# Row sums in SBUF, column mixing in one go, a later norm, a last tile in parts and a reordered first batch, in an attention-and-mixer kernel

## The chip, the cores and the metric

The kernel runs on one core of a Trainium2 chip. The metric is the device time of one execution in microseconds (us), as the median of several runs. Beside it stand profiles: one execution each, with every instruction of every engine. The engines are PE (matrix products), PEld (PE's weight loads), DVE (the vector engine), ACT (the scalar engine), POOL (GpSimd) and SP, which here only issues transfers. A profile's span is about 1.8 us shorter than the time of the same run, so spans are compared with spans and times with times.

Each run also lists its mean granted PE clock, where 1.000 is full speed.

## The reference, cut to what matters

Eight batches, each with 12 heads, 448 tokens and 64 numbers per head, so 768 columns per token:

```python
q_n, k_n = rmsnorm(q, g_q), rmsnorm(k, g_k)        # over the 64 numbers of a head
attn = softmax(q_n @ k_n^T / 8)
x    = heads side by side of attn @ v              # (8, 448, 768)
u    = x + (x^T @ U @ V)^T                         # "mixing": rank 32, over tokens
out  = u + relu(u @ w_ch1) @ w_ch2                 # "MLP": 768 -> 3072 -> 768
```

## The kernel before: the parts that matter

One stream of PE work carries everything. While PE makes the two MLP products of batch b (`ph`, then `po`), the pieces of batch b + 1 (scores, exponentials, values, then the mixing) are woven between its matmuls. Only batch 0 has no MLP to hide behind: its order is written out by hand in a string, HEAD. A "pair" is two heads of a batch; six pairs make a batch, so pairs 12 and 13 open batch 2.

Row sums of squares go into one PSUM bank. The logarithm and the exponential work in place there, and the scaling reads the result:

```python
rs_bank = ps_r.tile([SP, 6 * 16], FP32, name="rs_bank")      # PSUM
def reduce(p, hs=ALL):
    nc.vector.tensor_reduce(rs_of(p)..., sqs[p]..., AX, OP.add)
def rsqrt(p, n=1):
    rs = rs_of(p, n)
    nc.scalar.activation(rs, rs, AF.Ln, bias=eps)
    nc.scalar.activation(rs, rs, AF.Exp, scale=-0.5)
def scale(p):
    ...  # qkn = qk * rs_of(p), one DVE instruction of 112 x 1024
```

The mixing multiplies x by U in two column halves. In each, four matmuls of 32 output rows run side by side on four strips of the array (in the mixing of batch 3 they start within 0.01 us, from 230.39). All the large products share a pool of three PSUM buffers:

```python
ps_mm = ctx.enter_context(tc.tile_pool(name="ps_mm", bufs=3, space=bass.MemoryType.PSUM))
def mix_t(b, cols):
    t4 = t_of(b)
    for c in cols:
        pm = ps_mm.tile([P, c.stop - c.start], FP32, tag="mm", name="pm")
        mix_to(pm, b, c)
        nc.vector.tensor_copy(t4[:, c], pm)
def mixing(b):
    items = [(1, lambda h=h: mix_t(b, [slice(h * HALF, (h + 1) * HALF)])) for h in range(2)]
    for i in range(3 + b % 2):
        for half in range(2):
            items.append((1, lambda i=i, half=half: mix_x(b, i, half)))
    ...
```

The second MLP product writes 384 columns at a time, DVE adds x, and a whole tile of 128 tokens is stored at once on SP's queue:

```python
for i, half in order:
    po = ps_mm.tile([P, HALF], FP32, tag="mm", name="po")
    for hc in range(KH):                    # KH = 24
        nc.tensor.matmul(po, hT[:, hc, i * P:(i + 1) * P], w2b[:, half, hc], ...)
    nc.vector.tensor_add(osb[:, hs], po, xt[i][:, hs])
    if half == 1:
        store(b, off, off + P, osb, 0)      # two nc.sync.dma_start
```

The kernel begins with idle products on zeros, `heat(NWARM, ...)`, and HEAD has more of them (`F1:2` means one such product, into bank 2). The other words are steps too: `sq1:a` squares pair 1 on ACT, `R1` its row sums, `q1` its root, `S1` its scaling, `SC00` scores, `X00` an exponential.

The softmax here doesn't subtract the row's maximum and nothing guards it: scores larger than these inputs give would overflow.

Of the kernel before, what the change touches and what calls it, by code (L numbers as in the profile page):

```python
# [9 lines left out]
FP32 = mybir.dt.float32  # L10
# [7 lines left out]
def kernel(  # L18
# [20 lines left out]
    P = 128  # L39
# [14 lines left out]
    def segments(c0, c1):  # L54
        c = c0
        while c < c1:
            j, p = divmod(c, SP)
            n = min(SP - p, c1 - c)
            yield j, p, p + n, c - c0
            c += n  # L60
# [24 lines left out]
    eps = consts.tile([SP, 1], FP32, name="eps")  # L85
    rk0 = consts.tile([SP, 8], FP32, name="rk0")
    NE, NV, NQ, NWARM = 2, 3, 4, 12
    Es = [consts.tile([SP, 2, PAD + NJ * S + PAD], BF16, name=f"E{i}") for i in range(NE)]
# [11 lines left out]

    def rs_of(p, n=1):

        c = 16 * (p % 6)
        return rs_bank[:, c:c + 16 * n]

# [110 lines left out]
    def reduce(p, hs=ALL):  # L216
        nc.vector.tensor_reduce(rs_of(p).rearrange("p (s h j) -> p s h j", s=2, h=2)[:, :, hs],  # L217
                                sqs[p].rearrange("p (s h j d) -> p s h j d", s=2, h=2, d=D)[:, :, hs], AX, OP.add)

    def rsqrt(p, n=1):  # L220
        rs = rs_of(p, n)
        nc.scalar.activation(rs, rs, AF.Ln, bias=eps)
        nc.scalar.activation(rs, rs, AF.Exp, scale=-0.5)  # L223
# [103 lines left out]
    def t_of(b):  # L327
        if b not in t4s:
            t4s[b] = upool.tile([P, dm], BF16, tag="t4b", name="t4b", bufs=3)
        return t4s[b]  # L330

    def mix_to(pm, b, c):
        xt = x_tiles(b)
        for i in range(4):
            nc.tensor.matmul(pm[i * rank:(i + 1) * rank, :], Ub[:, b % 2, i, :], xt[i][:, c],  # L335
                             start=True, stop=True)

    def mix_t(b, cols):
        t4 = t_of(b)
        for c in cols:  # L340
            pm = ps_mm.tile([P, c.stop - c.start], FP32, tag="mm", name="pm")
            mix_to(pm, b, c)
            nc.vector.tensor_copy(t4[:, c], pm)
# [23 lines left out]
    def mixing(b):  # L367
        items = [(1, lambda h=h: mix_t(b, [slice(h * HALF, (h + 1) * HALF)])) for h in range(2)]
        for i in range(3 + b % 2):
            for half in range(2):  # L370
                items.append((1, lambda i=i, half=half: mix_x(b, i, half)))
            items.append((0, lambda i=i: turn_u(b, i)))
        return items

    def store(b, c0, c1, osb, r0):
        orow = out[b].rearrange("(p j) d -> j p d", j=NJ)
        for j, p0, p1, r in segments(c0, c1):
            nc.sync.dma_start(orow[j, p0:p1, :], osb[r0 + r:r0 + r + p1 - p0, :])

    def mlp(b):  # L380
# [19 lines left out]
        if b == 0:  # L400
            order = [(i, half) for half in range(2) for i in range(3)]
        for i, half in order:
            off = OFFS[par][i]
            if i not in osbs:
                osbs[i] = opool.tile([P, dm], FP32, tag="osb", name="osb")
            osb = osbs[i]
            hs = slice(half * HALF, (half + 1) * HALF)
            po = ps_mm.tile([P, HALF], FP32, tag="mm", name="po")
            for hc in range(KH):
                nc.tensor.matmul(po, hT[:, hc, i * P:(i + 1) * P], w2b[:, half, hc],  # L410
                                 start=(hc == 0), stop=(hc == KH - 1))
                if hc % 6 == 5 and hc != KH - 1:
                    yield HALF
            nc.vector.tensor_add(osb[:, hs], po, xt[i][:, hs])  # L414
            if half == 1:
                if off < 0:
                    store(b - 1, 384, 448, osb, 0)
                    store(b, 0, 64, osb, 64)
                else:
                    store(b, off, off + P, osb, 0)  # L420
            yield HALF

    def attention(b):
        items = []

        def add(weight, fn, *args):
            items.append((weight, lambda: fn(*args)))

        for p in range(b * 6, b * 6 + 6):
# [21 lines left out]
            if t + 2 < NT:  # L451
                for a in range(2):
                    if odd and p > 10:
                        add(0, reduce, 2 * t + 4 + a if p > 11 else 12 + a)
                    elif not odd and not early:
                        add(0, squares, 2 * t + 4 + a)
# [24 lines left out]
            if p == 9:  # L481
                add(0, touch, 6)
                add(0, load, 6)
                add(0, load_v, 6)
            if odd and p > 10 and t + 2 < NT:
                add(0, rsqrt, 2 * t + 4 if p > 11 else 12, 2)
        add(1, values, b * 6 + 5, 0)
# [24 lines left out]
    def begin(hcs, dcs):  # L512
# [17 lines left out]
    HEAD = """  # L530
        sq00:a R00 sq01:a q00 R01 q01 rk00 rk01 Sq00 G Sk0 Sq01 GC Tq0:0 Sl0 sq2:p Tk0:1 F1:2
        Tl0:2 sq3:p sq1:a Eq0 R1 Ek0:a SC00 F3:0 El0:v q1 cast0 S1 X00 SC01 F2:0 R2 sq4:p SC02
        T1:0 w10 X01 SC03 F3:1 X02 q2 Eq1 X03 Ek1:v w11 S2 SC10 F1:0 SC11 X10 T2:0 R3 SC12 late
        sq5:p X11 V01:1 Ek2:v Eq2 SC13 cast1 V00:0 q3 N01 X12 X13 w12 SC20 S3 X20 w13 SC21 T3:1
        R4 SC22 X21 sq6:p q4 V11:2 X22 SC23 Eq3 Ek3:v N00 V10:1 cast2 SC30 X23 S4 pU:0 N10 SC31
        N11 X30 X31 T4:1 R5 Ub:a SC32 V20:2 Eq4 SC33 X32 Ek4:v X33 q5 w14 N20 V21:0 N21 MT0:1
        SC40 X40 MT1:2 SC41 t1:a V31:0 t0:v MU0:1 S5 N31 X41 u0:v SC42 T5:2 X42 MT2:0 Eq5 SC43
        V30:1 Ek5:v SC50 X43 R6 t2:a MU1:2 SC51 X50 sq7:p N30 V40:0 X51 SC52 X52 u1:v MT3:1
        MU2:2 SC53 N40 X53 w15 V41:0 t3:v B10 R7 MU3:1 q6 u2:a u3:a N41 B00 V51:0 V50:2 B11
        MT4:1 w20 B01 B12 S6 t4:a N51 MU4:0 N50 MT5:1 w21 t5:a u4:a B02 B13 MU5:1 B03 u5:a S7  # L540
        B14 B04 B15 B05
    """

    def head():
# [3 lines left out]
        copies = {"a": nc.scalar.copy, "v": nc.vector.tensor_copy}  # L548
        rs0 = [rs_bank[:, 0:8], rsb[0:SP, 0, 0:8]]
        FIRST, REST = slice(0, 1), slice(1, NJ)  # L550

# [11 lines left out]
        def op(name, p, n, how):  # L563
# [5 lines left out]
            elif name == "R":  # L569
                if p == 0:  # L570
                    src = sqs[0].rearrange("p (s h j d) -> p s h j d", s=2, h=2, d=D)[:, :, n]
                    nc.vector.tensor_reduce(rs0[n].rearrange("p (s j) -> p s j", s=2), src, AX, OP.add)
                else:
                    reduce(p)
            elif name == "q" and p == 0:
                nc.scalar.activation(rs0[n], rs0[n], AF.Ln, bias=eps)
                nc.scalar.activation(rs0[n][:, 0:4], rs0[n][:, 0:4], AF.Exp, scale=-0.5)
# [85 lines left out]
    with tc.manual_schedule():  # L663
# [4 lines left out]
        load_pair(nc.sync, 0, 0, 1)  # L668
        load_pair(nc.scalar, 0, 1, 1)
        nc.scalar.preload_act_table_set("natural_log_exp_and_others")  # L670
# [15 lines left out]
        for b in range(B):  # L686
            fill = mlp(b)
            if b == 0:
# [12 lines left out]
                squares(15)  # L701
                weave(fill, volume(0) * 0.135, mixing(1))
                for a in range(2):
# [42 lines left out]
```

## Time and profile before

| | before |
|---|---|
| time, median of 3 runs | 593.5 us |
| span of the profile | 592.1 us |
| first `ph`, the start of batch 0's MLP | 39.67 us |
| first `po` row of 36 matmuls, just after the mixing of batch 1 | 98.39 us |
| last such row, just after the mixing of batch 7 | 519.02 us |

The last three rows are landmarks. The view of the critical chain joins neighbouring matmuls of one kind into a row, and after each mixing an unbroken row of 36 (odd batches) or 48 (even) `po` matmuls follows, so the start of this row tells to 0.01 us how far PE has come. They cut the span into the first batch, the stretch to the mixing of batch 1 (which holds the norm of batch 2), the steady part, and the tail.

Two more views of the kernel before, beside those that the prediction shows. First PE's waits, by what released them (columns: total us, times, longest), then the page's row of the wide row sums (busy us, mean ns of one, idle before them and its cause):

```profile
PE o L288 <- DVE xe L308: 1.5, 1, 1.5
PE sc L505 <- DVE xe L118: 1.3, 1, 1.3
PE sc L275 <- ACT qkT L250: 1.1, 1, 1.1
```

```profile
L217 DVE TENSOR_REDUCE rs_bank<-sq 112x16 f32<-112x1024 f32 x43 | 52.6, 1223 | 5.0 <-POOL sq L214 1.8
```

The first line is the wait in front of the mixing of batch 1. Its releaser is a small multiplication of DVE (it scales an output of the attention), but the second fence has the true cause: the row sums stood 1.8 us idle for squares of GpSimd, which had waited 1.85 us for a load.

### The profile page before, as it was taken

The numbers are of one execution on the slowest core, as the hardware profiler recorded it, in microseconds if no ns is written. First come the engines' busy times: TensorE is split into PE (matmuls) and PEld (weight loads), VectorE is DVE, ScalarE is ACT, GpSimd is POOL, SyncE is SP. The second block draws the span as 40 slices with busy tenths as digits, with TensorE's granted clock in tenths as the row PEclk, the third lists the DMA queues.
The fourth block names the chain that finished last, engine by engine and source line by source line (L and its number), as shares of the span: only waits on it lengthen the run. The fifth ranks groups of instructions, "written<-read, shape, count | busy, mean of one in ns | idle before, by whom it ended". The sixth has DMA issues, their size and how long they took to land.

```text
span 592.1 us, 11276 instructions
## 1 busy us (share of the span) xinstructions
PE 579.1 (98%) x4699; PEld 317.9 (54%) x4720; DVE 296.5 (50%) x599; ACT 263.3 (44%) x427; POOL 127.4 (22%) x112
## 2 busy tenths in 40 slices
PE   7999999999999999999999999999999999999996
PEld 3665555444655556544565556544565555554563
DVE  5967858454544566354453655454454452521111
ACT  6966530666305761366411774066620576113200
POOL 6946032333110332031130230302312000000000
PEclk9999999999999999999999999999999999999999
DMA  8999996925533445443154742641555210140011
GB/s 262 257 245 239 204 273 135 268 60 138 145 98 61 132 129 163 110 138 115 42 158 94 154 128 71 170 129 55 137 141 95 59 32 2 50 85 0 1 53 54
DMA packets 107955, 72.27 MB, mean 122 GB/s; under 512 B 56592, under 2 KB 104320, under 8 KB 107904
## 3 DMA queue, kind: packets, MB, share of 16 engines
q1 hardware_dynamic: 96336, 61.58, 39.8%
q0 software_dynamic: 11008, 9.44, 9.8%
q8 instruction: 37, 0.61, 0.4%
q10 hardware_dynamic: 560, 0.52, 0.3%
q14 instruction: 14, 0.11, 0.1%
HBM read 56.78 MB, written 11.01 MB: 114 GB/s over the span
## 4 chain that ended last, share of the span: by engine, by line
PE 91%; DMA 3%; DVE 3%; ACT 1%; issue 1%; SPq 0%; POOL 0%; DVEq 0%; POOLq 0%; ACTq 0%
PE ph L390 37%; PE po L410 36%; PE sc L275 7%; PE o L288 7%; DMA qk<-in_k_dram 2%; PE px L360 1%; DVE rs_bank L217 1%; DMA qk<-in_q_dram 1%; PE bank L288 1%; DVE qkn L228 1%; PE sc L520 1%; PE pm L335 1%; ACT E L280 0%; SPq L183 0%; ACT hT L393 0%
## 5 line engine op out<-in xcount | busy, mean ns | idle before, releaser
L280 ACT ACTIVATE E<-sc 112x896 bf16<-112x896 f32 x192 | 172.1, 914 | 157.0 <-PE sc L275 157.0
L410 PE MATMUL po<-w2b,hT 128*128 128x384 bf16 x1344 | 238.3, 326 | 0.0
L410 PEld LDWEIGHTS <-hT 128*128 128x128 bf16 x1344 | 126.4, 98 | 87.6 <-issue 9.0
L390 PEld LDWEIGHTS <-w1b 128*128 128x128 bf16 x1128 | 102.7, 98 | 105.2 <-issue 18.9
L214 POOL TENSOR_TENSOR sq<-qk 112x1024 f32<-112x1024 f32 x42 | 79.3, 1893 | 312.3 <-DMA qk<-in_k_dram 169.7
L390 PE MATMUL ph<-uB,w1b 128*128 128x512 bf16 x556 | 131.4, 379 | 1.1
L393 ACT ACTIVATE hT<-ph 128x512 bf16<-128x512 f32 (+1 forms) x122 | 66.7, 547 | 106.5 <-PE ph L390 106.0
L390 PE MATMUL ph<-uA,w1b 128*128 128x384 bf16 x552 | 100.3, 326 | 0.1
L395 DVE TENSOR_SCALAR hT<-ph 128x384 bf16<-128x384 f32 (+1 forms) x66 | 41.1, 622 | 90.4 <-PE ph L390 90.2
L288 PEld LDWEIGHTS <-E 112*128 112x128 bf16 x1536 | 60.8, 98 | 18.0 <-issue 3.2
L288 PE MATMUL o<-va,E 112*128 112x65 bf16 x1344 | 56.9, 194 | 1.5 <-DVE xe L308 1.5
L275 PE MATMUL sc<-qkT 64*128 64x448 bf16 x376 | 54.6, 355 | 1.6 <-ACT E L280 0.7
L228 DVE TENSOR_TENSOR qkn<-qk,rs_bank 112x1024 bf16<-112x1024 f32 x45 | 54.5, 1214 | 3.0 <-ACT rs_bank L223 2.6
L217 DVE TENSOR_REDUCE rs_bank<-sq 112x16 f32<-112x1024 f32 x43 | 52.6, 1223 | 5.0 <-POOL sq L214 1.8
L300 DVE RECIPROCAL rec<-o 128x4 f32<-128x4 f32 x84 | 15.2, 182 | 72.3 <-PE o L288 71.9
L414 DVE TENSOR_TENSOR osb<-po,xe 128x384 f32<-128x384 f32 x32 | 17.7, 557 | 40.2 <-PE po L410 39.6
L414 DVE TENSOR_TENSOR osb<-po,xo 128x384 f32<-128x384 f32 x24 | 13.4, 558 | 43.4 <-PE po L410 43.4
L275 PEld LDWEIGHTS <-qkT 64*128 64x128 bf16 (+1 forms) x384 | 13.3, 94 | 36.5 <-issue 28.2
L200 POOL CAST va<-vt 112x1024 bf16<-112x1024 f32 x23 | 23.9, 1040 | 2.7 <-DVE rs_bank L217 1.4
L266 ACT ACTIVATE qkT<-qkT,gg 128x448 bf16<-128x448 bf16 x36 | 23.8, 662 | 0.0
L362 DVE TENSOR_TENSOR xe<-px,xe 128x384 bf16<-128x384 f32 x32 | 17.7, 554 | 10.1 <-PE px L360 7.1
L308 DVE TENSOR_TENSOR xe<-o,rec 64x64 bf16<-64x64 f32 x84 | 18.3, 218 | 0.7
(92 smaller groups left out, 212.4 us busy)
## 6 DMA issues: line engine op xcount, KB each, us to landing
qk<-in_q_dram SPq DMA_DIRECT2D x44, 256.0 KB, 4.3
vt<-in_v_dram SPq DMA_DIRECT2D x22, 512.0 KB, 5.7
qk<-in_k_dram SPq DMA_DIRECT2D x43, 256.0 KB, 4.7
w1b<-in_moe_w_ch_dram POOLq DMA_DIRECT2D x6, 768.0 KB, 22.2
w2b<-in_moe_w_ch_dram POOLq DMA_DIRECT2D x6, 768.0 KB, 34.8
out_dram<-osb SPq DMA_DIRECT2D x8, 336.0 KB, 2.8
out_dram<-osb SPq DMA_DIRECT2D x8, 288.0 KB, 2.9
out_dram<-osb SPq DMA_DIRECT2D x8, 240.0 KB, 2.7
```

The source lines that it names most:

```text
L200: nc.gpsimd.tensor_copy(vas[t % NV][:, :, :, 0:D], v_of[t][0:SP].rearrange("p h (j d) -> p h j d", d=D))
L214: nc.gpsimd.tensor_tensor(dst, src, src, OP.mult)
L217: nc.vector.tensor_reduce(rs_of(p).rearrange("p (s h j) -> p s h j", s=2, h=2)[:, :, hs], sqs[p].rearrange("p (s h j d) -> p s h j d", s=2 ...
L228: nc.vector.tensor_tensor(qkns[p].rearrange("p j g d -> p g j d"), qk_of[t][0:SP, a].rearrange("p s h (j d) -> p (s h) j d", d=D), rs_of(p ...
L275: nc.tensor.matmul(sc[0:n, hh, 0:S], flat[pp, c:c + n], blocks(p)[pp, :, 0], start=True, stop=True)
L280: nc.scalar.activation(Es[p % NE][:, :, PAD + kc * S:PAD + (kc + 1) * S], scs.pop((p, kc))[0:SP, :, 0:S], AF.Exp, scale=float(D) ** 0.5)
L288: nc.tensor.matmul(o[:, i, :], E[:, hh, c:c + P], va[:, hl, kc, :], start=(kc == 0), stop=(kc == NJ - 1))
L390: nc.tensor.matmul(ph, w1b[:, dc, hc * P:(hc + 1) * P], u[:, dc, :], start=(dc == 0), stop=(dc == KD - 1))
L393: nc.scalar.activation(hT[:, hc, 0:n], ph, AF.Relu)
L395: nc.vector.tensor_relu(hT[:, hc, 0:n], ph)
L410: nc.tensor.matmul(po, hT[:, hc, i * P:(i + 1) * P], w2b[:, half, hc], start=(hc == 0), stop=(hc == KH - 1))
L414: nc.vector.tensor_add(osb[:, hs], po, xt[i][:, hs])
```

## The change

The intent has five parts, each of which removes a wait or shortens an end; no product is removed.

1. The row sums are written to an SBUF tile; the logarithm reads that and writes its result to the PSUM bank. A row sum no longer waits for the bank's other users (0.6 us in e3_sums_psum, which takes this part back), and a root no longer for the next pair's sum (2.05 us in e8_psum_heat).
2. The eight matmuls of a mixing run in one go, into two PSUM buffers.
3. The row sum of pair 13 and the root of pairs 12 and 13 move from the attention of batch 1 into its mixing.
4. The last 384 columns of the last tile become two parts of 192, so the last half tile is stored in parts, and two queues issue the stores.
5. HEAD has a new order, with SBUF sums as its condition.

```diff
+    sums = consts.tile([SP, 6 * 16], FP32, name="sums")
     def reduce(p, hs=ALL):
-        nc.vector.tensor_reduce(rs_of(p)...
+        nc.vector.tensor_reduce(rs_of(p, of=sums)...
     def rsqrt(p, n=1):
-        nc.scalar.activation(rs, rs, AF.Ln, bias=eps)
+        nc.scalar.activation(rs, rs_of(p, n, sums), AF.Ln, bias=eps)
     def mix_t(b, cols):
         for c in cols:
-            pm = ps_mm.tile(...)
-            mix_to(pm, b, c)
+            pms.append(ps_mm.tile(...))
+            mix_to(pms[-1], b, c)
+        for c, pm in zip(cols, pms):
             nc.vector.tensor_copy(t4[:, c], pm)
     # attention of batch 1, pair 11
-                    if odd and p > 10:
-                        add(0, reduce, 2 * t + 4 + a if p > 11 else 12 + a)
+                    if odd and p > 11 or p == 11 and a == 0:
+                        add(0, reduce, 2 * t + 4 + a if p > 11 else 12)
     # mixing of batch 1
+                items[3:3] = [(0, lambda: reduce(13)), (0, lambda: rsqrt(12, 2))]
     # mlp
+        if b == B - 1:
+            parts[-1:] = [(3, 1, 0, HALF // 2), (3, 1, HALF // 2, HALF)]
+            if last:
+                store(b, off, off + P, osb, 0, cols, (nc.sync, nc.scalar))
     # first two lines of HEAD, of eleven
-        sq00:a R00 sq01:a q00 R01 q01 rk00 rk01 Sq00 G Sk0 Sq01 GC Tq0:0 Sl0 sq2:p Tk0:1 F1:2
-        Tl0:2 sq3:p sq1:a Eq0 R1 Ek0:a SC00 F3:0 El0:v q1 cast0 S1 X00 SC01 F2:0 R2 sq4:p SC02
+        sq00:a sq01:a R00 q00 R01 q01 rk00 rk01 sq1:a Sq01 Sk0 G GC Sl0 Sq00 Tk0:0 F2:1 Tl0:1
+        sq2:a Tq0:2 sq3:p Ek0:a El0:a R1 Eq0 q1 sq4:p SC00 R2 SC01 F2:0 X00 SC02 F1:0 cast0 S1
     # cut: the rest of HEAD, weights of the mixing's items, one load on the other queue
```

More of the change, by code (lines that the diff above doesn't have):

```diff
@@ L99, with rs_of @@
     rs_bank = ps_r.tile([SP, 6 * 16], FP32, name="rs_bank")
-    def rs_of(p, n=1):
+    def rs_of(p, n=1, of=rs_bank):
         c = 16 * (p % 6)
-        return rs_bank[:, c:c + 16 * n]
+        return of[:, c:c + 16 * n]
     spare = hT.rearrange("p k n -> p (k n)").bitcast(FP32)
@@ L216, in reduce @@
     def reduce(p, hs=ALL):
-        nc.vector.tensor_reduce(rs_of(p).rearrange("p (s h j) -> p s h j", s=2, h=2)[:, :, hs],
+        nc.vector.tensor_reduce(rs_of(p, of=sums).rearrange("p (s h j) -> p s h j", s=2, h=2)[:, :, hs],
                                 sqs[p].rearrange("p (s h j d) -> p s h j d", s=2, h=2, d=D)[:, :, hs], AX, OP.add)
@@ L338, in mix_t @@
     def mix_t(b, cols):
-        t4 = t_of(b)
+        t4, pms = t_of(b), []
         for c in cols:
-            pm = ps_mm.tile([P, c.stop - c.start], FP32, tag="mm", name="pm")
-            mix_to(pm, b, c)
+            pms.append(ps_mm.tile([P, c.stop - c.start], FP32, tag="mm", name="pm"))
+            mix_to(pms[-1], b, c)
+        for c, pm in zip(cols, pms):
             nc.vector.tensor_copy(t4[:, c], pm)
@@ L367, in mixing, with store @@
     def mixing(b):
-        items = [(1, lambda h=h: mix_t(b, [slice(h * HALF, (h + 1) * HALF)])) for h in range(2)]
+        items = [(1, lambda: mix_t(b, [slice(h * HALF, (h + 1) * HALF) for h in range(2)]))]
         for i in range(3 + b % 2):
             for half in range(2):
-                items.append((1, lambda i=i, half=half: mix_x(b, i, half)))
+                items.append((1 if i or half else 2, lambda i=i, half=half: mix_x(b, i, half)))
             items.append((0, lambda i=i: turn_u(b, i)))
         return items
-    def store(b, c0, c1, osb, r0):
+    def store(b, c0, c1, osb, r0, cols=slice(0, dm), engines=(nc.sync, nc.sync)):
         orow = out[b].rearrange("(p j) d -> j p d", j=NJ)
-        for j, p0, p1, r in segments(c0, c1):
-            nc.sync.dma_start(orow[j, p0:p1, :], osb[r0 + r:r0 + r + p1 - p0, :])
+        for n, (j, p0, p1, r) in enumerate(segments(c0, c1)):
+            engines[n].dma_start(orow[j, p0:p1, cols], osb[r0 + r:r0 + r + p1 - p0, cols])
     def mlp(b):
@@ L401, in mlp @@
             order = [(i, half) for half in range(2) for i in range(3)]
-        for i, half in order:
+        parts = [(i, half, 0, HALF) for i, half in order]
+        if b == B - 1:
+            parts[-1:] = [(3, 1, 0, HALF // 2), (3, 1, HALF // 2, HALF)]
+        for i, half, w0, w1 in parts:
             off = OFFS[par][i]
+            last = b == B - 1 and i == 3
             if i not in osbs:
@@ L406, in mlp @@
             osb = osbs[i]
-            hs = slice(half * HALF, (half + 1) * HALF)
-            po = ps_mm.tile([P, HALF], FP32, tag="mm", name="po")
+            cols = slice(half * HALF + w0, half * HALF + w1)
+            po = ps_mm.tile([P, w1 - w0], FP32, tag="mm", name="po")
             for hc in range(KH):
-                nc.tensor.matmul(po, hT[:, hc, i * P:(i + 1) * P], w2b[:, half, hc],
+                nc.tensor.matmul(po, hT[:, hc, i * P:(i + 1) * P], w2b[:, half, hc, w0:w1],
                                  start=(hc == 0), stop=(hc == KH - 1))
                 if hc % 6 == 5 and hc != KH - 1:
-                    yield HALF
-            nc.vector.tensor_add(osb[:, hs], po, xt[i][:, hs])
-            if half == 1:
+                    yield w1 - w0
+            nc.vector.tensor_add(osb[:, cols], po, xt[i][:, cols])
+            if last:
+                store(b, off, off + P, osb, 0, cols, (nc.sync, nc.scalar))
+            elif half == 1:
                 if off < 0:
@@ L420, in mlp @@
                     store(b, off, off + P, osb, 0)
-            yield HALF
+            yield w1 - w0
     def attention(b):
@@ L484, in attention @@
                 add(0, load_v, 6)
-            if odd and p > 10 and t + 2 < NT:
-                add(0, rsqrt, 2 * t + 4 if p > 11 else 12, 2)
+            if odd and p > 11 and t + 2 < NT:
+                add(0, rsqrt, 2 * t + 4, 2)
         add(1, values, b * 6 + 5, 0)
@@ L530 @@
     HEAD = """
-        sq00:a R00 sq01:a q00 R01 q01 rk00 rk01 Sq00 G Sk0 Sq01 GC Tq0:0 Sl0 sq2:p Tk0:1 F1:2
-        Tl0:2 sq3:p sq1:a Eq0 R1 Ek0:a SC00 F3:0 El0:v q1 cast0 S1 X00 SC01 F2:0 R2 sq4:p SC02
-        T1:0 w10 X01 SC03 F3:1 X02 q2 Eq1 X03 Ek1:v w11 S2 SC10 F1:0 SC11 X10 T2:0 R3 SC12 late
-        sq5:p X11 V01:1 Ek2:v Eq2 SC13 cast1 V00:0 q3 N01 X12 X13 w12 SC20 S3 X20 w13 SC21 T3:1
-        R4 SC22 X21 sq6:p q4 V11:2 X22 SC23 Eq3 Ek3:v N00 V10:1 cast2 SC30 X23 S4 pU:0 N10 SC31
-        N11 X30 X31 T4:1 R5 Ub:a SC32 V20:2 Eq4 SC33 X32 Ek4:v X33 q5 w14 N20 V21:0 N21 MT0:1
-        SC40 X40 MT1:2 SC41 t1:a V31:0 t0:v MU0:1 S5 N31 X41 u0:v SC42 T5:2 X42 MT2:0 Eq5 SC43
-        V30:1 Ek5:v SC50 X43 R6 t2:a MU1:2 SC51 X50 sq7:p N30 V40:0 X51 SC52 X52 u1:v MT3:1
-        MU2:2 SC53 N40 X53 w15 V41:0 t3:v B10 R7 MU3:1 q6 u2:a u3:a N41 B00 V51:0 V50:2 B11
-        MT4:1 w20 B01 B12 S6 t4:a N51 MU4:0 N50 MT5:1 w21 t5:a u4:a B02 B13 MU5:1 B03 u5:a S7
-        B14 B04 B15 B05
+        sq00:a sq01:a R00 q00 R01 q01 rk00 rk01 sq1:a Sq01 Sk0 G GC Sl0 Sq00 Tk0:0 F2:1 Tl0:1
+        sq2:a Tq0:2 sq3:p Ek0:a El0:a R1 Eq0 q1 sq4:p SC00 R2 SC01 F2:0 X00 SC02 F1:0 cast0 S1
+        X01 R3 q2 w10 T1:0 X02 q3 SC03 F3:1 Eq1 Ek1:v late cast1 S2 S3 X03 w11 SC10 F1:0 SC11
+        T2:0 X10 X11 Ek2:v SC12 V01:1 SC13 X12 X13 w12 Eq2 V00:2 SC20 N01 X20 R4 T3:0 SC21 Eq3
+        pU:1 X21 SC22 Ek3:v sq5:p q4 N00 V11:0 X22 Ub:v SC23 X23 V10:1 S4 N10 SC30 T4:2 X30 SC31
+        MT0:1 N11 Eq4 MT1:0 t0:v SC32 cast2 X31 V21:1 Ek4:v t1:a SC33 X32 V20:0 R5 X33 N21 SC40
+        N20 q5 X40 MU0:2 SC41 MT2:0 S5 V30:1 u0:v t2:a X41 w13 SC42 N30 T5:0 Eq5 MU1:2 sq6:p
+        SC43 V31:1 Ek5:v sq7:p X42 u1:v SC50 MU2:0 X43 X50 SC51 V40:2 N31 u2:a R6 X51 SC52 N40
+        MT3:0 X52 t3:v V41:1 w14 SC53 w15 MU3:0 N41 B00 MT4:1 B01 X53 u3:a R7 q6 V51:2 t4:v N51
+        V50:0 B10 MU4:1 B11 B02 N50 S7 MT5:0 u4:a B12 t5:a B03 MU5:0 w20 B13 u5:a B04 w21 S6 B14
+        B05 B15
     """
@@ L549, in head @@
         rs0 = [rs_bank[:, 0:8], rsb[0:SP, 0, 0:8]]
+        sums0 = [sums[:, 0:8], sums[:, 8:16]]
         FIRST, REST = slice(0, 1), slice(1, NJ)
@@ L571, in op @@
                     src = sqs[0].rearrange("p (s h j d) -> p s h j d", s=2, h=2, d=D)[:, :, n]
-                    nc.vector.tensor_reduce(rs0[n].rearrange("p (s j) -> p s j", s=2), src, AX, OP.add)
+                    nc.vector.tensor_reduce(sums0[n].rearrange("p (s j) -> p s j", s=2), src, AX, OP.add)
                 else:
@@ L575, in op @@
             elif name == "q" and p == 0:
-                nc.scalar.activation(rs0[n], rs0[n], AF.Ln, bias=eps)
+                nc.scalar.activation(rs0[n], sums0[n], AF.Ln, bias=eps)
                 nc.scalar.activation(rs0[n][:, 0:4], rs0[n][:, 0:4], AF.Exp, scale=-0.5)
@@ L668 @@
         load_pair(nc.sync, 0, 0, 1)
-        load_pair(nc.scalar, 0, 1, 1)
+        load_pair(nc.sync, 0, 1, 1)
         nc.scalar.preload_act_table_set("natural_log_exp_and_others")
@@ L701 @@
                 squares(15)
-                weave(fill, volume(0) * 0.135, mixing(1))
+                items = mixing(1)
+                items[3:3] = [(0, lambda: reduce(13)), (0, lambda: rsqrt(12, 2))]
+                weave(fill, volume(0) * 0.135, items)
                 for a in range(2):
```

## The prediction

> **What bounds the kernel now.** I read the page's busy shares and the chain that ended last, then a table of engine time by stretch, then the timeline wherever the matrix engine (PE) was not full. First the page:
>
> ```profile
> PE 579.1 (98%) x4699; PEld 317.9 (54%) x4720; DVE 296.5 (50%) x599; ACT 263.3 (44%) x427; POOL 127.4 (22%) x112
> ...
> PE 91%; DMA 3%; DVE 3%; ACT 1%; issue 1%; SPq 0%; POOL 0%; DVEq 0%; POOLq 0%; ACTq 0%
> ```
>
> PE is busy for 579.1 of 592.1 us and carries 91% of the last chain. The change removes no matrix product, so its gain must come from the 13.0 us in which PE is not busy, or from pauses that the record hides (a matmul counts as busy until its modelled end, so pauses up to some 0.2 us don't show). Where are the 13 us? In the table, columns after the length are PE, PEld, DVE, ACT, POOL busy us, clock, DMA share, GB/s:
>
> ```profile
> 0.00:10.00 10.00, 7.61 (x30) 3.11 (x30) 4.10 (x7) 4.89 (x12) 5.61 (x26) 1.00 0.79 246
> 10.00:20.00 10.00, 8.13 (x92) 4.42 (x92) 9.38 (x14) 9.21 (x16) 9.83 (x12) 1.00 0.95 284
> 20.00:30.00 10.00, 9.33 (x160) 6.42 (x157) 9.80 (x25) 9.72 (x18) 9.72 (x9) 1.00 1.17 248
> ...
> 80.00:90.00 10.00, 8.54 (x105) 5.45 (x102) 6.47 (x16) 3.49 (x6) 5.06 (x4) 1.00 1.12 291
> ...
> 300.00:400.00 100.00, 99.78 (x811) 55.83 (x813) 52.34 (x103) 41.73 (x67) 20.55 (x13) 1.00 0.50 126
> ...
> 580.00:592.10 12.10, 7.15 (x45) 4.11 (x42) 1.12 (x2) 0.00 (x0) 0.00 (x0) 0.94 0.23 65
> ```
>
> There are three holes: the first 30 us miss 2.39 + 1.87 + 0.67 = 4.93 us, the stretch 80 to 90 misses 1.46, the end misses 4.95. They make 11.3 of the 13.0. In the middle 100 us miss 0.2. In the first hole VectorE (DVE) has 9.38 and 9.80 us of work in 10, ScalarE nearly as much: batch 0 runs as fast as those two. The second hole on the timeline:
>
> ```profile
> 84.43 1.89 POOL L214 TENSOR_TENSOR sq<-qk 112x1024 f32<-112x1024 f32 x1 [1.85 <-DMA qk<-in_k_dram]
> ...
> 86.35 1.23 DVE L217 TENSOR_REDUCE rs_bank<-sq 112x16 f32<-112x1024 f32 x1 [1.76 <-POOL sq L214]
> ...
> 88.49 0.69 PE L288 MATMUL o<-va,E 112*128 112x65 bf16 x16 [1.46 <-DVE xe L308]
> ```
>
> A late load holds GpSimd, that holds the row sum of pair 13 (batch 2), this stands first in DVE's queue, and PE waits behind it for a PSUM buffer. The mixing in steady state, here of batch 3:
>
> ```profile
> 230.39 0.34 PE L335 MATMUL pm<-xe,Ub 128*32 128x384 bf16 x1
> 230.40 0.34 PE L335 MATMUL pm<-xo,Ub 128*32 128x384 bf16 x3
> 230.50 0.56 DVE L414 TENSOR_TENSOR osb<-po,xe 128x384 f32<-128x384 f32 x1 [0.16 <-PE po L410]
> ...
> 230.67 1.15 PE L410 MATMUL po<-w2b,hT 128*128 128x384 bf16 x6
> ...
> 231.75 0.34 PE L335 MATMUL pm<-xe,Ub 128*32 128x384 bf16 x1
> 231.75 0.34 PE L335 MATMUL pm<-xo,Ub 128*32 128x384 bf16 x3
> ```
>
> Four matmuls start together on four column strips. The rest of the timeline has a 384-column matmul every 0.162 us, yet here 0.28 us pass until the next `po`, and 0.11 before (230.67 + 6 x 0.162 = 231.64 to 231.75): 0.39 us for 0.16 of streaming. The end:
>
> ```profile
> 587.19 0.56 DVE L414 TENSOR_TENSOR osb<-po,xo 128x384 f32<-128x384 f32 x1 [3.34 <-PE po L410]
> ```
>
> then two store issues on the SP queue, 0.78 us together from 587.78, landing up to 2.8 us after issue, and the end of the span at 592.1.
>
> [...] The trace has 1223 ns for 1024 elements[...]. The row sum reads SBUF already; no trace shows yet what its target costs. [...]
>
> **Part by part.** *Row sums in SBUF.* The 47 wide sums keep DVE 57.5 us (52.6 + 4.9). [...] Its true use is freedom of order[...]. I book it under batch 0.
>
> *Mixing in one go.* [...] Two groups cost 2 x 0.39 = 0.78; eight matmuls at a time cost 0.11 + 0.16 + 0.28 = 0.55: 0.23 saved. But the pool has three PSUM buffers, and now two are `pm` at once. In the even batches an open `po` has the third and all goes on: 3 x 0.23 = 0.7 us. In the odd batches (1, 3, 5, 7) the mixing falls on the border of two `po`, and in the changed order the next `po` waits for the addition that empties the old one. That ends at 230.50 + 0.56 = 231.06, with 0.06 of signalling 231.12, where PE would be free at 230.39 + 0.16 + 0.28 = 230.83. The 0.29 lost eats the 0.23: 4 x +0.06. Sum -0.5 us.
>
> *Norm of batch 2 later.* Sum 13 and the pair's root move behind the first two `px`. By then (past 93 us) its squares, ready at 86.3, have long been there, so the 1.46 us hole goes. But 1.2 us enters DVE's queue among the `px` additions. DVE then reaches the additions of px 3 and 4 about 0.6 us late, and the next `po`, which needs px 4's buffer, starts about that much later. Net 1.5 - 0.7 = -0.8 us.
>
> *Last tile.* The last addition has 192 columns for 384: 357 ns (the row of 192-column normalisations) for 557, -0.2. The last store issue doesn't stand behind another, -0.36. It carries 84 KB for 336: stores of 96 KB land in 2.3 us, those of 336 KB in 2.8, -0.5. PE's work stays: 48 x 0.081 for 24 x 0.162. Sum -1.05 us.
>
> *Batch 0.* From the first row sum of pair 1 (8.92) to the end of the last scaling (37.63) DVE spans 28.7 us with about 1.2 idle. The new order gives DVE +0.41 (Ub) and +0.28 (a t4 copy), takes 0.32 (a K copy)[...]: no shorter, unless the idle 1.2 goes. ScalarE gets more ahead of its first exponential: squares of pair 2 (1.06) and the K copy, so I walk that to 11.4 instead of 10.54; from there 24 exponentials at 0.833 and the smaller work need 22.65 instead of 22.97. The last exponential is then 0 to 0.6 later, but after it the two normalisations don't stand behind a 1.21 us scaling as at 34.19, which brings the last mixing forward by about 1. Sum -0.7, between -2 and +0.5. One heating matmul less hides in it.
>
> Sum: -0.5 - 0.8 - 1.05 - 0.7 = -3.05. With a little for hidden pauses I say 590.2.
>
> **Rivals.** *DMA holds the start.* To 90 us the DMA share is 1.0 to 1.3. The weights land one after another (w2's third part at 71.1, used at about 73.6; its last at 89.1, used at 94). They were queued long before, so the later issue costs nothing, but an earlier PE meets them with 2.5 us of slack. If more than that is saved before 70 us, it comes back as a wait; pair 12's row sum may likewise wait for its load. For it: the shares; against: no wait of PE on a weight now. Worth up to +1.5: 591.7. *The odd batches' wait is longer* than 0.29 (DVE's queue full at that moment): +0.2 each, 591. *Batch 0 was the true aim* and both DVE and ScalarE get denser: -2.5 instead of -0.7, 588.4. For it: 4.9 us of PE are empty there; against: DVE's 9.80 of 10. *The later norm costs all it saves*: +0.7, 590.9.
>
> **Range and chances.** The tail is surest (0.3 either way), batch 0 least (1.3), the norm 0.5, mixing 0.5. Their root of squares is 1.5; 8 in 10 needs about 1.3 of these, some 2.1. So 588.0 to 592.3. Two per cent would need 11.9 us, more than all three holes together (11.3), of which 3 to 4 us at each end are loads and landing that stay. I give faster 0.02. Slower would need something unseen: 0.01.
>
> **What would show it.** Tail: from the last addition's end to the span's end about 3.5 us (now 4.35), an addition of about 0.36. Norm: no wait of `o` on `xe` near 87, sum 13 with no idle before it, a pause of 0.5 or more soon after. Mixing: eight `pm` together; in odd batches the next `po` about 0.7 after the first `pm`, in even ones 0.45. [...] Batch 0: the first `ph` (39.67 now) between 38 and 40. I am wrong if PE shows new waits on DMA between 65 and 95 us, or if the first `ph` moves by over 2 us.

The sum came to -3.05 us. An estimate of up to 0.45 us for shorter row sums in batch 0 was no term of the sum, as batch 0's -0.7 rests on the normalisations after the last exponential. The figures that the text leaves without a source are in the trace of the kernel before: an issue of the last two stores took 0.36 us (0.32 and 0.41), the 0.06 of signalling passes between the end of the `xe` multiplication at 88.43 and the matmul at 88.49, and the up to 0.2 us of pause that a record can hide come from matmuls of 384 columns that are recorded with 0.34 us and start every 0.162. The 3 to 4 us at each end are an estimate, from the first square at 3.64 us and the 4.35 after the last addition.

## The result, and the profile after

The changed kernel took 590.36 us (median of 4 runs, 589.37 to 590.95); in the same rounds the kernel before took 593.65. The ratio is 0.9943, with a 95% interval of 0.9926 to 0.996: within 2%, as expected, and 0.16 us from the predicted time. Ratios here are the mean time of one kernel's fast runs over that of the other's of the same rounds, so not quite the ratio of the medians quoted.

| landmark (us) | before | after | gain from the landmark above |
|---|---|---|---|
| first `ph` | 39.67 | 39.39 | 0.28 |
| first `po` row of 36, batch 1 | 98.39 | 96.79 | 1.32 |
| last `po` row of 36, batch 7 | 519.02 | 516.86 | 0.56 |
| end of the span | 592.1 | 588.3 | 1.64 |

The four gains add up to the 3.8 us between the spans. The page after answers to the one before (busy shares, the chain that ended last, the row sums):

```profile
PE 580.0 (99%) x4743; PEld 319.5 (54%) x4743; DVE 294.4 (50%) x601; ACT 264.2 (45%) x427; POOL 125.6 (21%) x111
...
PE 95%; DVE 2%; ACT 1%; DMA 1%; issue 0%; SPq 0%; DVEq 0%; ACTq 0%
...
L218 DVE TENSOR_REDUCE sums<-sq 112x16 f32<-112x1024 f32 x43 | 50.5, 1208 | 1.3 <-ACT sq L213 1.0
```

PE is as busy as before in a shorter span, and its part of the chain rose from 91 to 95%. A row sum fell by 15 ns only. PE's waits after:

```profile
PE sc L276 <- DVE qkT L248: 1.6, 1, 1.6
PE sc L513 <- DVE xe L119: 1.3, 1, 1.3
PE po L416 <- DVE osb L420: 0.8, 4, 0.2
```

The wait of `o` on `xe` is gone, and four new ones of `po` on an addition have come, one for each odd batch. The first line will matter. The table by stretch after (columns as in the prediction):

```profile
0.00:10.00 10.00, 6.68 (x28) 2.91 (x28) 4.33 (x8) 6.22 (x15) 4.99 (x26) 0.95 0.85 264
10.00:20.00 10.00, 10.00 (x84) 4.44 (x84) 8.95 (x13) 8.42 (x16) 8.90 (x11) 0.71 1.04 313
...
80.00:90.00 10.00, 9.79 (x118) 6.24 (x117) 6.47 (x18) 2.61 (x4) 6.72 (x4) 1.00 0.97 280
```

From 80 to 90 us PE's empty time fell from 1.46 to 0.21 us. From 10 to 20 us PE went from 8.13 to 10.00 busy, which looks like a great gain and is none: it has 84 matmuls there against 92, and the clock column fell from 1.00 to 0.71. The same matmuls took longer: two scores of pair 0 0.62 us (at 11.76) against 0.40 before (at 11.51), eight transposes 0.95 (at 12.72) against 0.57 (at 11.94). The prediction had not foreseen this, and several of the experiments below are about it.

The mixing of batch 3 and the tail after, from the timeline:

```profile
228.56 0.34 PE L336 MATMUL pm<-xe,Ub 128*32 128x384 bf16 x1
228.56 0.34 PE L336 MATMUL pm<-xo,Ub 128*32 128x384 bf16 x3
228.67 0.56 DVE L420 TENSOR_TENSOR osb<-po,xe 128x384 f32<-128x384 f32 x1 [0.16 <-PE po L416]
228.73 0.33 PE L336 MATMUL pm<-xe,Ub 128*32 128x384 bf16 x1
228.74 0.33 PE L336 MATMUL pm<-xo,Ub 128*32 128x384 bf16 x3
...
229.28 1.14 PE L416 MATMUL po<-w2b,hT 128*128 128x384 bf16 x6 [0.21 <-DVE osb L420]
```

```profile
585.09 0.36 DVE L420 TENSOR_TENSOR osb<-po,xo 128x192 f32<-128x192 f32 x1 [1.62 <-PE po L416]
```

The two groups of four start 0.17 us apart, and the next `po` comes 0.72 after the first. It waits for the addition that began at 228.67 and ended at 229.23. From the last addition's end (585.45) to the end of the span are 2.85 us, where it was 4.35.

### The profile page after: what moved, and what is told of

Same layout as the page of the kernel before. It is cut to its first block, busy times and chain, and to the rows that moved or that the text cites. A ratio compares the mean times of both kernels' runs of the same rounds, so it can differ in the third digit from the quotient of the medians.

```text
span 588.3 us, 11324 instructions
## 1 busy us (share of the span) xinstructions
PE 580.0 (99%) x4743; PEld 319.5 (54%) x4743; DVE 294.4 (50%) x601; ACT 264.2 (45%) x427; POOL 125.6 (21%) x111
## 4 chain that ended last, share of the span: by engine, by line
PE 95%; DVE 2%; ACT 1%; DMA 1%; issue 0%; SPq 0%; DVEq 0%; ACTq 0%
PE po L416 37%; PE ph L392 37%; PE sc L276 8%; PE o L289 7%; PE px L362 1%; PE bank L289 1%; DMA qk<-in_k_dram 1%; PE sc L528 1%; PE bank L513 1%; DVE osb L420 0%; ACT E L281 0%; DVE sums L218 0%; PE pt L244 0%; ACT hT L395 0%; DVE qkT L248 0%
## 5 line engine op out<-in xcount | busy, mean ns | idle before, releaser
L416 PE MATMUL po<-w2b,hT 128*128 128x384 bf16 (+1 forms) x1368 | 237.8, 323 | 1.0 <-DVE osb L420 0.8
L416 PEld LDWEIGHTS <-hT 128*128 128x128 bf16 x1368 | 128.5, 98 | 88.3 <-issue 11.0
L229 DVE TENSOR_TENSOR qkn<-qk,rs_bank 112x1024 bf16<-112x1024 f32 x45 | 54.3, 1213 | 3.5 <-ACT rs_bank L224 3.4
L218 DVE TENSOR_REDUCE sums<-sq 112x16 f32<-112x1024 f32 x43 | 50.5, 1208 | 1.3 <-ACT sq L213 1.0
L420 DVE TENSOR_TENSOR osb<-po,xo 128x384 f32<-128x384 f32 (+1 forms) x25 | 13.5, 542 | 43.1 <-PE po L416 43.1
```

The lines of the kernel that those rows point to most:

```text
L218: nc.vector.tensor_reduce(rs_of(p, of=sums).rearrange("p (s h j) -> p s h j", s=2, h=2)[:, :, hs], sqs[p].rearrange("p (s h j d) -> p s h ...
L229: nc.vector.tensor_tensor(qkns[p].rearrange("p j g d -> p g j d"), qk_of[t][0:SP, a].rearrange("p s h (j d) -> p (s h) j d", d=D), rs_of(p ...
L420: nc.vector.tensor_add(osb[:, cols], po, xt[i][:, cols])
```

## The experiments

Twelve runs in three calls, each call on one chip together with eleven runs of the kernel before (medians 593.91, 594.08 and 594.01). Times are compared within a call, landmarks across all. My theory was the sum of the prediction's parts, plus one new claim: in batch 0 a pause of PE (1.64 us in the first profile) brings its clock from 1.00 to 0.50, and that takes back what the new order gains. The rivals were that the half clock is chance and has nothing to do with the change, that batch 0 gains nothing because DVE bounds it, and that the later norm or the second queue does nothing.

### The changed kernel once more: c0_after

> The changed kernel again, as the base of this call. Theory 'clock': in its profile the granted TensorE clock is 0.50 from about 9 to 15.6 us; if that comes from PE standing still from 8.2 to 9.7 us it shows in every run, as a mean clock of 0.993 to 0.997 where the kernel before has 0.999. Rival 'chance': the state of the clock is drawn anew in each run and the kernel before has it as often; then some runs here show 0.999 and some of before 0.994. Time expected 589.4 to 591.0.

589.42 us (588.76 to 589.81, 6 runs), ratio 0.9922 [0.9909, 0.9935]. The profile has a span of 588.0, a first `ph` at 39.17 and again a clock of 0.994. All ten runs of the changed kernel have 0.993 to 0.997. Of 33 runs of the kernel before, 11 have 0.999 or 1.0 (mean 593.66 us), 8 have 0.997 or 0.998 (594.15) and 14 have 0.996 or less (594.63). So a lower mean clock is not new: the kernel before has one in two runs of three, and by these means is up to 1 us slower then. The changed kernel had one in ten runs of ten. That spells of half clock lie behind all of these is an estimate, from the spell in its first profile and the run's mean of 0.994 there.

### Six heating products in the pause: e1_heat6

```diff
-        sq2:a Tq0:2 sq3:p Ek0:a ...
+        sq2:a Tq0:2 W6 sq3:p Ek0:a ...
+            elif name == "W":
+                heat(p, warm[:, 0, :])
```

> Six heating matmuls more, put where PE stands still between the transposes of pair 0 and its first scores (8.2 to 9.7 us). Theory 'clock': the granted clock stays 1.00 through the first 20 us, the first exponentials follow each other as in the kernel before, and the first matmul of the MLP comes 0.5 to 1.5 us earlier (38 to 38.9 for 39.4); time 589.0 to 589.8 and less scatter. Rival 'the half clock is hidden': scalar and vector engine bound batch 0 anyway; the clock goes to 1.00 but the first MLP matmul stays at 39.2 to 39.5 and the time at 590.3. Rival 'chance': clock still 0.994.

588.95 us (588.05 to 589.15, 6 runs), ratio 0.9912 [0.9898, 0.9927], and every run at 0.999 or 1.0. Tables of two us each show what the products do. The changed kernel without them:

```profile
8.00:10.00 2.00, 0.36 (x7) 0.34 (x4) 1.83 (x3) 1.71 (x6) 0.12 (x1) 0.74 1.06 354
10.00:12.00 2.00, 2.00 (x8) 0.50 (x7) 2.00 (x3) 1.83 (x5) 1.77 (x1) 0.50 1.09 384
12.00:14.00 2.00, 2.00 (x13) 1.01 (x11) 1.48 (x3) 1.74 (x6) 1.22 (x1) 0.50 1.05 250
14.00:16.00 2.00, 2.00 (x8) 0.44 (x6) 2.00 (x4) 0.92 (x1) 2.00 (x3) 0.55 0.96 290
```

And with them:

```profile
8.00:10.00 2.00, 1.88 (x15) 0.70 (x12) 1.65 (x3) 1.61 (x4) 0.04 (x1) 1.00 1.04 355
10.00:12.00 2.00, 1.73 (x12) 0.68 (x10) 1.95 (x3) 1.97 (x5) 1.85 (x1) 1.00 1.09 384
12.00:14.00 2.00, 1.66 (x15) 0.73 (x13) 2.00 (x4) 1.90 (x6) 1.13 (x1) 1.00 0.91 234
14.00:16.00 2.00, 1.91 (x21) 0.95 (x20) 2.00 (x2) 2.00 (x4) 2.00 (x3) 1.00 0.90 273
```

Without them PE is busy for 0.36 us between 8 and 10, and then stays full at clock 0.50 until 15.8, so that even the few matmuls of this stage take all of its time. With them the clock stays at 1.00, and between 14 and 16 us 21 matmuls get done instead of 8. The pause itself is on the timeline of the changed kernel, the first of its waits listed above:

```profile
9.87 1.00 PE L276 MATMUL sc<-qkT,qkT 64*112 64x448 bf16 x4 [1.64 <-DVE qkT L248]
```

The first `ph` comes at 37.92 against 39.17, so 1.25 us earlier. The medians differ by only 0.47, and the intervals of the ratios overlap, as five of c0_after's six runs are at 0.997, and the profiled one at 0.994. That filling the pause keeps the clock and brings batch 0 forward is shown; its average worth is below what one profile says.

In the first profile of the changed kernel the clock is 0.50 from 9.0 to 15.8 us. It fell when PE had stood still for 0.8 us, and between 5 and 9 us PE was busy for 2.87 us of 4.00. In c0_after the whole pause is 1.26 us long, and the clock fell at 9.0 as well.

So the fall comes around the pause (in six of the profiles PE's clock is 0.50 for some 6.8 us around a pause of PE of 1.26 to 1.87 us in batch 0), and with the pause filled all six runs are at 0.999 or 1.0, but what exactly sets it off is not shown. The profiles of the old order have 0.98 to 1.10 us of pause in this place and a clock of 1.00, and around the wait of 1.46 us at 87 us the kernel before has 1.00, too. One more thing differs from a plain pause and was not tested: from 7.6 us to the end of the pause PE makes nothing but seven transposes.

### The old order of batch 0: e2_old_head

The eleven lines of HEAD, and the one load that changed queues, as before; everything else changed.

> The changed kernel with batch 0 in the order of before (and the fourth load on the queue of before); all other parts stay. By the traces the first MLP matmul moved by 0.28 us only. Theory 'the new order is worth little because of the half clock': the clock is full again, first MLP matmul at 39.3 to 39.7[...], time 590.2 to 590.8, so within 0.4 of the changed kernel. Rival 'the order matters': time 591.5 or more. Rival 'sums in SBUF alone do it': first MLP matmul below 39.2.

590.10 us (589.5 to 590.4, 6 runs), ratio 0.9933 [0.992, 0.9945]. The profile has clock 1.0, a span of 588.0 and the first `ph` at 39.14: the very landmark that the new order reaches at half clock. So the forecast of the third rival (SBUF sums alone, below 39.2) came true for the landmark. The time is 0.68 us above c0_after, where I had expected 0.4 at most, but the intervals of the two ratios overlap.

The absolute landmark moves with the loads (the first exponential lies between 9.74 and 10.93 us), so I also took the interval from the first exponential to the first `ph`. It repeats better: four profiles of the new order at half clock have 28.86 to 29.04. It is 28.54 us here and 28.54 in e9_sums_only, 29.13 in the kernel before and 29.12 in e10_before_heat, 29.04 in c0_after and 27.70 in e1_heat6 (27.69 in e11_best). Read in this order: SBUF sums in the old order give 0.59, the new order at full clock another 0.84, and the half clock takes 1.2 to 1.3 of it back.

### Row sums back in PSUM: e3_sums_psum

```diff
+    sums = rs_bank
-        sums0 = [sums[:, 0:8], sums[:, 8:16]]
+        sums0 = rs0
```

> The changed kernel with the row sums back in the PSUM tile, where logarithm and exponential work in place. Theory 'freedom of order': in the new order of batch 0 a row sum then waits for the root of another pair in the same bank, so batch 0 gets longer by 0.5 to 2 us, and steady state is the same. Rival 'only cost': each sum goes from 1208 back to 1223 ns, 7 in batch 0, 0.1 us, no change of the first MLP matmul beyond 0.2.

591.24 us (590.89 to 591.99, 6 runs), ratio 0.9954 [0.9941, 0.9967]: 1.8 us slower than with the sums in SBUF. A row sum took 1222 ns against 1208. Seven sums at 14 ns are 0.1 us, so the cost of the instruction explains little of this. A wait of the kind that I expected is there, but small: four sums stood 0.6 us idle, in all, for the exponential of another pair's root. The first `ph` came 1.28 us later (40.45 against 39.17), both at half clock; the interval from the first exponential is 0.79 us longer (29.83 against 29.04). Part of the 1.8 us may be clock: five of the six runs here are at 0.994, one of c0_after's.

### The same at full clock: e8_psum_heat

e3_sums_psum with the six heating products of e1_heat6.

> The new order of batch 0 with the row sums in PSUM and the clock kept up by six heating matmuls. It parts the two: without heating the PSUM sums cost 1.28 us to the first MLP matmul (40.45 for 39.17), but there the half clock also lasted to 17 us for 15.6. Theory 'waits in the bank': with a full clock still 0.5 to 1.3 us later than the heated kernel with SBUF sums (37.92), so 38.4 to 39.2. Rival 'the clock did it': 37.9 to 38.2.

592.66 us (590.33 to 593.01, 6 runs), ratio 0.9964 [0.9948, 0.9981]. The profile fell on a run at clock 1.0, and its first `ph` is at 39.54, later than I had expected. The interval from the first exponential is 29.60 against 27.70: at full clock the new order with PSUM sums loses 1.90 us. The table of two us shows what is lost, against the same lines of e1_heat6 above:

```profile
12.00:14.00 2.00, 1.65 (x13) 0.75 (x13) 1.90 (x4) 0.25 (x2) 1.55 (x1) 1.00 1.11 280
14.00:16.00 2.00, 0.69 (x3) 0.37 (x4) 0.98 (x3) 1.97 (x5) 2.00 (x3) 1.00 1.10 321
```

ACT stands almost empty from 12 to 14 (0.25 us for 1.90) and DVE for half of 14 to 16. The timeline has the wait, that of the root of pair 2:

```profile
13.71 0.25 ACT L223 ACTIVATE rs_bank<-rs_bank,eps 112x16 f32<-112x16 f32 x1 [2.05 <-DVE rs_bank L218]
```

The sum of pair 2 had ended at 11.03; what the root waits for is the sum of pair 3, which goes into the same bank. In e1_heat6 these two run side by side (root at 11.87, sum from 11.89). Nothing but the target of the sums differs. So what SBUF sums are worth is the freedom to run a sum while the bank is in use; with PSUM sums the new order is worse than the old.

The times of the six runs go with the clock: 590.33 us at clock 1.0, 591.05 at 0.999, 592.49 at 0.997, and 592.83 to 593.01 at 0.994. Heating at one place was not enough here: four of these six runs fell to 0.997 or less. Where their clock fell is not on record, as the profile caught a run at 1.0.

### SBUF sums alone, in the kernel before: e9_sums_only

> The kernel before with the row sums in SBUF as its only change. The changed kernel with the old order has its first MLP matmul at 39.14, the kernel before at 39.67. Theory 'SBUF sums give 0.5 in the old order too': first MLP matmul at 39.0 to 39.3, time -0.4 to -0.7. Rival 'something else of the change': 39.5 to 39.7 and no gain. Each sum 1208 ns for 1223 in both.

593.44 us (592.48 to 594.53, 5 runs), ratio 0.9987 [0.9973, 1.0002], so not separable from the kernel before in time. In the trace the interval in batch 0 is shorter by 0.59 us, a little more than the 0.45 that I had as the most.

### Three heating products in the kernel before: e10_before_heat

```diff
-        Tl0:2 sq3:p sq1:a Eq0 R1 ...
+        Tl0:2 W3 sq3:p sq1:a Eq0 R1 ...
```

> The kernel before with three heating matmuls more in its gap at 8.0 to 9.1 us. Its clock is full already. Theory 'heating pays only by the clock': no change beyond 0.2 us. Rival 'an earlier or fuller matrix engine helps by itself': -0.5 or more.

593.46 us (593.05 to 594.83, 5 runs), ratio 0.9994 [0.9979, 1.0009]. Four of five runs have 0.999 or 1.0, against two of eleven of the kernel before. So with heating the lower clocks seem to be rarer there too (on few runs), without a gain that the interval could hold. The first `ph` came 0.8 us earlier, but so did the first exponential, and the interval between them is unchanged: that landmark moved with the loads.

### The norm back in its old place: e4_old_norm

```diff
-                    if odd and p > 11 or p == 11 and a == 0:
-                        add(0, reduce, 2 * t + 4 + a if p > 11 else 12)
+                    if odd and p > 10:
+                        add(0, reduce, 2 * t + 4 + a if p > 11 else 12 + a)
-                items[3:3] = [(0, lambda: reduce(13)), (0, lambda: rsqrt(12, 2))]
```

> The changed kernel with the row sum of pair 13 and the root of pairs 12 and 13 back where they were, in the attention of batch 1. By the traces the move took away a stop of 1.63 us near 87 and gave back 0.47 between 88 and 97, of which some 0.04 belong to the mixing. Theory: time +1.2 us, the wait of o on xe near 87 is back. Rival from the prediction: 0.7 given back, so +0.8. Rival 'the load would no longer be late': now that batch 0 is shorter the load lands earlier against the row sum; +0.3 or less.

591.29 us (589.08 to 591.9, 6 runs), ratio 0.9945 [0.9928, 0.9961]. The wait is back, with the size that it had before:

```profile
88.07 0.69 PE L289 MATMUL o<-va,E 112*128 112x65 bf16 x16 [1.45 <-DVE xe L309]
```

From the first `ph` to the `po` row after the mixing of batch 1 it needs 58.61 us against 57.40 in c0_after, so the later norm is worth 1.21. A landmark between the two splits this: up to the first mixing matmul it saves 1.64 us (50.25 to 48.61), and from there it gives 0.43 back (8.36 to 8.79). The row sum now stands among the `px` additions with no idle time before it, and its 1.21 us pushes the work behind it:

```profile
92.00 1.21 DVE L218 TENSOR_REDUCE sums<-sq 112x16 f32<-112x1024 f32 x1
...
93.13 1.01 DVE L364 TENSOR_TENSOR xo<-px,xo 128x384 bf16<-128x384 f32 x2
```

Against c0_after, the medians say 1.9 rather than 1.2 and the ratios 1.4, with another mix of clocks: four of its six runs at 0.994, against one of c0_after's six. Its one run at 1.0 took 589.08.

### One queue for the last stores: e5_one_queue

```diff
-                store(b, off, off + P, osb, 0, cols, (nc.sync, nc.scalar))
+                store(b, off, off + P, osb, 0, cols)
```

> The changed kernel with both stores of each part of the last tile on the SP queue. Theory: the second queue saves one issue, so +0.32 to +0.38 us at the end and nothing else. Rival 'the small stores bring it all': the time stays within 0.1. From the last addition's start to the span's end 3.5 us for 3.2.

590.06 us (588.71 to 590.56, 6 runs), ratio 0.9929 [0.9916, 0.9941]. Times do not separate it from the changed kernel. In the trace the end comes 3.10 us after the last addition, against 2.78 in c0_after and 2.85 in the first profile. The second queue is thus worth 0.3 us, about the 0.36 of one issue (the median of this run's four last ones).

### A fourth PSUM buffer in place of the bank: e6_four_banks

The four waits of `po` on an addition (0.8 us together) I put down to the pool's three buffers. To give it a fourth I moved the roots to SBUF as well and took their bank:

```diff
-    ps_mm = ... bufs=3
-    ps_r = ctx.enter_context(tc.tile_pool(name="ps_r", bufs=1, space=PSUM))
-    rs_bank = ps_r.tile([SP, 6 * 16], FP32, name="rs_bank")
+    ps_mm = ... bufs=4
+    rs_bank = consts.tile([SP, 6 * 16], FP32, name="rs_bank")
```

> The changed kernel with the root's results in SBUF too, so that their PSUM bank becomes a fourth buffer for the matmul results. Theory 'the third buffer is what the odd batches wait for': the four waits of po on osb (0.8 us) vanish, each odd batch gains the full 0.23 like the even ones (0.27 better each, 1.1 us in all), and the 0.43 us given back after the later norm shrinks; time -1.0 to -1.5. [...] Batch 0 may change by 0.3 either way.

595.25 us (594.06 to 595.47, 5 runs), ratio 1.0015 [1.0002, 1.0027]: slower than the kernel before, and my expectation missed. The part that it was meant for did come: the next `po` starts 0.44 us after the first mixing matmul, now in an odd batch too (234.70 after 234.26), with no wait for the addition. Between the first and the last `po` row of 36 that gained 0.8 us (419.28 against 420.06 in c0_after). But batch 0 lost some 6 us. Most of the reason is in three lines of its timeline:

```profile
22.73 4.80 DVE L228 TENSOR_TENSOR qkn<-hT,rs_bank 112x1024 bf16<-112x1024 f32 x1
...
23.15 1.91 POOL L214 TENSOR_TENSOR w2b<-hT 112x1024 f32<-112x1024 f32 x1
...
27.59 0.65 PE L243 MATMUL bank<-shift,qkn 112*128 112x112 bf16 x5 [3.72 <-DVE qkn L228]
```

A scaling that took 1.21 us now took 4.80, stretched over GpSimd's squares and the cast and the issue of a transfer that followed them, and PE waited 3.72 us for it. Around this second pause the clock fell once more (0.86 from 20 to 30 us and 0.80 from 30 to 40, which at a clock of 0.50 makes a spell from 27.2 to 34.0), and all five runs are at 0.988. The mean of 45 such scalings rose from 1213 to 1496 ns. Another one, which began at 11.25 while squares of 10.42 ran on GpSimd, took 2.15 us. In the changed kernel, with the roots in PSUM, a scaling beside the same squares took 1.22 us (at 21.41, the squares from 21.00), and here one (at 33.0) with nothing but issues of transfers on GpSimd beside it took 1.22 as well. So neither the squares nor the new place alone lengthened a scaling, but the two together; how they hold each other up was not shown. This may also be why the change moves the sums to SBUF and leaves the roots, which the scalings read, in PSUM.

### Both: e7_heat_banks

> The changed kernel with six heating matmuls and with four buffers. If the two gains are independent, the sum of both: about -0.5 to -1.2 and -1.0 to -1.5, so 587.0 to 588.0 us in rounds where the changed kernel has 589.4 to 590.4.

593.76 us (593.27 to 594.95, 6 runs), ratio 0.9996 [0.9985, 1.0008], so this expectation missed by about 6 us. The same slow scalings make PE wait 4.2 us on `qkn`, and around that wait the clock falls (0.79 from 20 to 30 us, 0.87 from 30 to 40), although it was at 1.00 for the first 20 us. It adds little beyond e6_four_banks: the fourth buffer is not to be had this way.

### The mixing moved by one group in odd batches: e11_best

Heating as in e1_heat6, and in the odd batches the mixing shifted by half a `po` (other weights in the weaving), so that it no longer falls on the border of two:

```diff
+        late = (1.5, 1.0, 0.9, 0.2, 0.9, 0.9, 0.2, 0.7, 0.18)
-        items = [(1, lambda: mix_t(...))]
+        items = [(late[0] if b % 2 else 1, lambda: mix_t(...))]
-            due += w * total / max(weights, 1)
+            due += w * total / weights
```

> The changed kernel with six heating matmuls, and in the odd batches the mixing one group of six matmuls later, so that the old po is drained before both pm take their buffers. Theory: each odd batch gains what the even ones do, 0.27 better, 4 of them 1.1 us, against the heated kernel (588.95 when the changed one had 589.4): 587.6 to 588.2. Rival 'the vector engine falls behind, as the products before the first px are packed closer': within 0.4 of the heated kernel.

588.74 us (588.4 to 588.92, 4 runs), ratio 0.9907 [0.9894, 0.992]. It is the fastest of all: surely faster than the kernel before, and below the changed kernel's 589.42 and 590.36. They were run at other times. Yet it is above the 587.6 to 588.2 that I had expected. The steady part gained what it should: 419.27 us against 420.06, or 0.26 for each of three odd batches, and `po` follows the mixing of batch 3 after 0.44 us. The mixing of batch 1 gave half of it back, with a wait that was not there:

```profile
93.60 1.14 PE L417 MATMUL po<-w2b,hT 128*128 128x384 bf16 x6 [0.94 <-DVE xo L364]
```

There the delayed norm meets the shifted additions: from the first `ph` to the `po` row it took 57.79 us against 57.41 in e1_heat6. Against e1_heat6 some 0.2 us stay by medians, from another chip, so that this last step is not separable from nothing in time.

## Why the prediction was right, point by point

**Tail** (predicted -1.05, measured -1.64). The addition fell by 0.2 us as worked out (0.36 measured), and the issue by about 0.3. The landing was mis-sized: I took 2.3 us from stores of 96 KB, but the last store of 84 KB landed in 1.8, against 2.8 for the 336 KB before. That gives 1.0 where I booked 0.5, and about 0.1 of the 1.64 stays unassigned. The lists of the last stores have the two landings, the first line from the kernel before and the second from the changed one:

```profile
out_dram<-osb SPq DMA_DIRECT2D x1, 336.0 KB, 2.8
...
out_dram<-osb ACTq DMA_DIRECT2D x2, 84.0 KB, 1.8
```

The kernel before had shown it, too: in the same list of it, 96 KB on a quiet queue landed in 1.8. Only the second queue was tested by itself (e5_one_queue).

**Later norm** (predicted -0.8, measured -1.2). The hole went (1.64 us, with the 1.46 of the wait in it), the sum ran without idle time, and the price appeared where foreseen. It was 0.43 instead of 0.7: again the mechanism was right and one term too large. The rival that the norm costs all it saves is refuted by e4_old_norm.

**Mixing** (predicted -0.5, measured -0.56 on the stretch with three even and three odd batches). Each even batch gained 0.23 us as worked out (75.59 to 75.36 between the rows around it). Each odd one lost 0.04, where +0.06 was foreseen, by the wait that was foreseen, and e11_best and e6_four_banks both removed it. No run takes back the single mixing alone, but SBUF sums in the old kernel leave an even batch at 75.59 (e9_sums_only), and the changed kernel with the old order or the old norm has 75.36. The rival of a longer wait didn't come: 0.21 us, four times.

**Batch 0** (predicted -0.7, measured -0.28) is the part whose steps failed, though the range held it. Three things were wrong. The first exponential was walked to 11.4 us and came at 10.53. SBUF sums were priced by their length too, by an estimate that no trace showed; measured are 15 ns less for each (1223 to 1208). Their worth lies in the order that they allow, and for that the prediction gave no size: e3_sums_psum shows 0.6 us of row sums waiting for a root, and e8_psum_heat a root on ACT that waits 2.05 us for the row sum of another pair. And the clock was taken as given. "One heating matmul less hides in it" was the whole of what I said on it, while around the pause that the new order leaves there (1.26 to 1.66 us in four profiles) the clock fell to 0.50 for 6.8 us. At full clock batch 0 gained 1.43 us (29.13 to 27.70 in the interval), and the half clock took back 1.16 in this profile. So at full clock batch 0 lies between the 0.7 that I booked and the 2.5 of the rival "batch 0 was the true aim".

**Rivals.** "DMA holds the start" did not come: no PE wait on a weight appears.

The sum came out at 590.2 against 590.36 measured. Part of that is luck: tail and norm gave 1.0 more than booked, and batch 0 gave 0.4 less in the profiles, while the times as medians fell by 3.3 where the spans fell by 3.8. **Open** stays where in the kernel before the clock falls, as its profile is of a run at 0.999, and how often a lower clock costs 1 us rather than 2: the kernel before lost about 1 at 0.996 and below, while the six runs of e8_psum_heat span 2.7.

## What to carry to other kernels

When a reordering changes when PE pauses, check the clock column of the windows before reading the busy column: here PE was suddenly full (10.00 us of 10 for 8.13) with fewer matmuls (84 for 92) at a clock of 0.71, and had gained nothing. A few idle products in the pause may bring back what the reordering lost (here 1.2 to 1.3 us of batch 0 in the profiles, 0.5 us in the medians). Moving a small operand between PSUM and SBUF changed little in the instruction itself (1223 to 1208 ns for a row sum); ask instead what the other instructions on the same bank waited for (here 2.05 us), and with whom the operand's new readers now collide (a scaling took 4.80 us for 1.21). Take the landing of a small last store from stores of its size on an equally quiet queue (here 1.8 us for 96 KB before and for 84 KB after).
